# An inverse of 32 x 32 triangles moved from VectorE to TensorE, with more word buffers and a third load queue

## Chip, cores, metric

One core of a Trainium2 chip. The metric is the device time of one execution in microseconds (us). Ratios are the mean time of one kernel's fast runs over the mean of the other's from the same rounds, on the same chip, so they are not quite the ratio of the medians that stand beside them. Stretches within a kernel are read from one profiled execution each; whole times of one kernel differ by some 5 us either way between executions, so differences of a few us in a stretch are not read as effects.

Engine names as in the profile: PE is TensorE (matmuls), PEld its weight loads, DVE VectorE, ACT ScalarE, POOL GpSimd, SP SyncE. "issue" in a wait is time in which an engine waited for nothing that the profile shows.

## The reference, cut to what matters

```python
# block 1, for every token t of 768, 4 x 8 heads of 40 channels
y[t]  = r[t] @ state
Sa    = state @ a[t]
state = state * w[t] - outer(Sa, b[t]) + outer(v[t], k[t])
# block 2, on x = y laid out as (3072 tokens, 320)
h = x @ w_in            # 320 x 2048, given in double precision
out = (h * cos(h)) @ w_out
```

The kernel takes block 1 in 24 chunks of 32 tokens. In a chunk the recurrence becomes matmuls and the inverse of a 32 x 32 unit triangular matrix for each head. The weights of block 2 arrive as pairs of 32-bit words and are turned into f32 on the chip ("conversion", 36 blocks). Block 2's matmuls are laid between the chunks from chunk 2 on.

## The kernel before: what the change touches

The inverse of four chunks at once, 31 steps of two operations on VectorE:

```python
def inv_step(j):
    u, x = (G[n].rearrange("p (s t) -> p s t", s=C) for n in ("u", "inv"))
    tmp = ...
    nc.vector.tensor_tensor(tmp, u[:, :j, j : j + 1].to_broadcast([P, j, C - j]),
                            x[:, j : j + 1, j:].to_broadcast([P, j, C - j]), ALU.mult)
    nc.vector.tensor_tensor(x[:, :j, j:], x[:, :j, j:], tmp, ALU.subtract)
```

One block of conversion is a fetch from POOL, five operations on VectorE and two on ScalarE, cut into four steps (fetch, exponent, mantissa, product) that are laid between the segments of the chunks. Three word buffers rotate (`sb3`). The order ahead of the main loop:

```python
for seg in (v, k, g, *other[3:]):   # chunk 0's operands, then the triangles of chunks 2 and 3
    step(seg)
for work in inverse(0):             # the inverse of chunks 0 to 3, alone on VectorE
    work()
...
segs = [x, v, extra[0], s, k, extra[1], z, g, *extra[2:]]   # chunk 0; s is the first to use the inverse
```

## Time and profile before

| | before |
|---|---|
| median (4 runs) | 940.8 us (937.7 to 946.2) |
| profiled span | 937.8 us |
| PE busy | 775 us, 16472 matmuls |
| DVE busy | 537 us |
| instruction packets (queue q8) | 130, 2.13 MB |

How to read it: PE is the bound from about 213 us on; ahead of that DVE is the busier engine, with PE half idle. The lines of the page and of the stretches are in the prediction. I use these marks throughout, all read from PE's timeline: the first matmuls on the inverse (tile sps, 74.0 us before) and the first state transpose of chunks 1 to 5 (tile sT; chunk 5 at 274.8).

### The profile page before, as it was taken

Reading aid. Unit: us, or ns where it says so; the run is one execution under the profiler, and the core shown is the slowest. Engines: PE = TensorE matmul, PEld = TensorE weight load, DVE = VectorE, ACT = ScalarE, POOL = GpSimd, SP = SyncE. Lnnn points to the kernel's source line nnn. Section 1 sums busy time; section 2 is a strip of 40 time slices with the busy share of each in tenths; the row PEclk is TensorE's granted clock in tenths of the full one; section 3 lists DMA queues with packets and bytes.
Section 4 is the critical chain, followed back from the end, with each engine's and each line's share of the span. In section 5 each row is a group of like instructions: output and inputs, shape, how many; then the busy total and the mean of one; then the engine's idle time right before and its main releaser. Section 6 shows DMA issues by size and latency. Waiting matters only on the chain.

```text
span 937.8 us, 36893 instructions
## 1 busy us (share of the span) xinstructions
PE 775.1 (83%) x16472; PEld 598.6 (64%) x16472; DVE 536.5 (57%) x1178; ACT 357.0 (38%) x671; POOL 189.3 (20%) x372
## 2 busy tenths in 40 slices
PE   5604554758899899989889999999898999999997
PEld 4404443546677667777667777777676676777675
DVE  5499787797723567726468526588334765323322
ACT  1103433543433433534324443433434344534333
POOL 4303333131211122112022013023102202211000
PEclk9655555778999889999989999999999899999999
DMA  5432636230311411421420421312211112200000
GB/s 95 82 49 66 151 93 147 74 89 2 69 46 23 74 44 20 73 55 27 69 46 16 72 50 38 61 39 49 57 33 38 32 25 47 45 19 24 18 22 15
DMA packets 181471, 49.08 MB, mean 52 GB/s; under 512 B 159040, under 2 KB 179008, under 8 KB 181312
## 3 DMA queue, kind: packets, MB, share of 16 engines
q1 hardware_dynamic: 176192, 35.89, 20.0%
q0 software_dynamic: 2944, 10.49, 3.6%
q8 instruction: 130, 2.13, 0.9%
q10 hardware_dynamic: 2176, 0.33, 0.2%
q14 instruction: 29, 0.24, 0.1%
HBM read 38.80 MB, written 7.86 MB: 50 GB/s over the span
## 4 chain that ended last, share of the span: by engine, by line
PE 64%; DVE 18%; issue 6%; DMA 5%; ACT 4%; SPq 2%; POOL 1%; POOLq 0%; ACTq 0%; DVEq 0%
PE ph L101 24%; PE po L101 19%; PE x0ps L101 4%; DVE inv_tmp L384 3%; PE dps L101 3%; DVE inv L388 3%; DVE rw L330 2%; PE gram L101 2%; DVE turns L620 2%; SPq L149 2%; PE qps L101 2%; PE vT L273 2%; PE sT L468 2%; PE sps L101 2%; ACT turns L618 2%
## 5 line engine op out<-in xcount | busy, mean ns | idle before, releaser
L101 PE MATMUL po<-w_out_sb,gT 128*128 128x320 f32 x768 | 243.6, 465 | 0.0
L101 PE MATMUL ph<-xT,w_in_sb 128*128 128x256 f32 x768 | 193.2, 396 | 13.9 <-DVE gT L628 6.2
L620 DVE SCALAR_TENSOR_TENSOR turns<-turns,ph 128x512 f32<-128x512 f32 x96 | 61.7, 684 | 219.8 <-ACT turns L618 219.8
L101 PEld LDWEIGHTS po<-w_out_sb,gT 128*128 128x128 f32 x768 | 148.7, 203 | 58.5 <-issue 13.3
L101 PEld LDWEIGHTS ph<-xT,w_in_sb 128*128 128x128 f32 x768 | 143.1, 195 | 36.0 <-issue 13.3
L618 ACT ACTIVATE turns<-ph,rnd 128x512 f32<-128x512 f32 x96 | 60.8, 684 | 146.4 <-PE ph L101 146.4
L558 POOL TENSOR_TENSOR qz<-qz,wc 128x160 f32<-128x160 f32 x92 | 41.7, 470 | 346.0 <-DVE qz L557 345.3
L628 DVE TENSOR_TENSOR gT<-ph,turns 128x512 f32<-128x512 f32 x96 | 65.0, 684 | 18.3 <-ACT turns L625 18.0
L384 DVE TENSOR_TENSOR inv_tmp<-u,inv 128x31 f32<-128x31 f32 (+15 forms) x186 | 71.8, 386 | 4.2 <-POOL inv L371 0.4
L388 DVE TENSOR_TENSOR inv<-inv,inv_tmp 128x31 f32<-128x31 f32 (+15 forms) x186 | 69.5, 374 | 6.4
L625 ACT ACTIVATE turns<-turns,half_pi 128x512 f32<-128x512 f32 x96 | 69.3, 722 | 3.1
L624 ACT ACTIVATE turns<-turns 128x512 f32<-128x512 f32 x96 | 60.0, 625 | 8.4 <-DVE turns L620 8.4
L101 PE MATMUL ph<-xT,w_in_tail 64*128 64x256 f32 x384 | 54.8, 404 | 0.0
L330 DVE RECIPROCAL rw<-wn 128x320 f32<-128x320 f32 x24 | 51.6, 2150 | 2.1 <-PE wn L273 2.1
L101 PEld LDWEIGHTS ph<-xT,w_in_tail 64*128 64x128 f32 x384 | 33.3, 187 | 18.4 <-issue 15.6
L472 ACT COPY s<-sT 128x512 f32<-128x512 f32 x46 | 24.6, 588 | 46.1 <-PE sT L468 46.1
L273 PE MATMUL wT<-ident,nat_w 128*128 128x128 f32 x88 | 14.4, 315 | 32.2 <-DVE x L509 25.3
L557 DVE TENSOR_TENSOR qz<-dps,qz 128x160 f32<-128x160 f32 x92 | 29.1, 317 | 19.1 <-PE dps L101 19.0
L530 DVE TENSOR_TENSOR sm<-sps,su 128x128 f32<-128x128 f32 x48 | 14.0, 291 | 45.1 <-ACT sm L526 45.1
L273 PE MATMUL bT<-ident,bn 128*128 128x128 f32 x96 | 18.6, 327 | 25.3 <-ACT bT L343 18.7
L202 ACT ACTIVATE expo<-expo,to_bits 128x256 int32<-128x256 int32 (+1 forms) x36 | 19.2, 533 | 49.6 <-DVE expo L199 49.4
L468 PE MATMUL sT<-ident,qz 128*128 128x128 f32 x184 | 26.5, 288 | 11.4 <-DVE aT L332 11.4
(104 smaller groups left out, 1082.9 us busy)
## 6 DMA issues: line engine op xcount, KB each, us to landing
words<-in_moe_w_out_dram POOLq DMA_DIRECT2D x16, 320.0 KB, 3.7
words<-in_moe_w_in_dram POOLq DMA_DIRECT2D x16, 256.0 KB, 3.5
nat_k<-in_k_dram SPq DMA_DIRECT2D x96, 40.0 KB
nat_v<-in_v_dram SPq DMA_DIRECT2D x96, 40.0 KB
nat_r<-in_r_dram SPq DMA_DIRECT2D x96, 40.0 KB
xd<-yt SPq DMA_DIRECT2D x48, 80.0 KB
out_dram<-ot SPq DMA_DIRECT2D x24, 160.0 KB
nat_w<-in_w_dram SPq DMA_DIRECT2D x88, 40.0 KB
```

Of the source, the lines that this page charges most:

```text
L101: nc.tensor.matmul(o, lhsT=lhsT, rhs=rhs, start=start, stop=stop, skip_group_check=True)
L273: nc.tensor.transpose(ps[:, i * P : (i + 1) * P], x[:, 2 * i : 2 * i + 2].rearrange("p e d -> p (e d)"), ident)
L330: nc.vector.reciprocal(rw, unpad(ps[:, 0].rearrange("p (h d) -> p h d", h=H)))
L384: nc.vector.tensor_tensor(tmp, u[:, :j, j : j + 1].to_broadcast([P, j, C - j]), x[:, j : j + 1, j:].to_broadcast([P, j, C - j]), ALU.mult,)
L388: nc.vector.tensor_tensor(x[:, :j, j:], x[:, :j, j:], tmp, ALU.subtract)
L468: nc.tensor.transpose(ps[:, i // 4, (i % 4) * P : (i % 4 + 1) * P], qz[:, i // 2, i % 2, C : C + P], ident)
L558: nc.gpsimd.tensor_tensor(z, z, wc.rearrange("p (f m b) -> p f m b", f=2, m=2)[:, :, :, bb] .unsqueeze(3).to_broadcast([P, 2, 2, D]), ALU. ...
L618: nc.scalar.activation(n, u, ACTF.Identity, bias=rnd, scale=1.0)
L620: nc.vector.scalar_tensor_tensor(n, n, -ROUND, u, ALU.add, ALU.subtract)
L624: nc.scalar.activation(n, n, ACTF.Abs)
L625: nc.scalar.activation(n, n, ACTF.Sin, bias=half_pi, scale=-2.0 * math.pi)
L628: nc.vector.tensor_tensor(gT[:, 2 * e : 2 * e + 2].rearrange("p f t -> p (f t)"), us[e], ns[e], ALU.mult)
```

## The change

Its intent: get the 28 us of the first inverse off VectorE, so that conversion can begin earlier. The inverse of chunks 0 to 3 is made by repeated squaring, (1 + u)(1 + u^2)(1 + u^4)(1 + u^8)(1 + u^16), with u and its transpose l squared on TensorE. Conversion gets five word buffers (two of them in the still empty end of the w_out tile). The loads of a and b for chunks 2 and 3 go over POOL's queue. The padding memsets go to VectorE. The core of the diff:

```diff
+    def doubled(c, n):
+        u, l, q = (G[x][:, c * H : (c + 2) * H] for x in ("nt", "l", "q"))
+        work = [] if n == 4 else [("l", u, l)] if n == 3 else [("u", l, u), ("l", u, l)]
+        ...
+        for i, (_, left, right) in enumerate(work):
+            for h in range(2 * H):
+                for g in blk:
+                    mm(ps[g, i, h * C : (h + 1) * C], left[g, h, :], right[g, h, :], h == 0)
+        if n:
+            for g in blk:
+                mm(qps[g], ident[g, g], flat(q[g]), True)
+            for h in range(2 * H):
+                for g in blk:
+                    mm(qps[g, h * C : (h + 1) * C], l[g, h, :], q[g, h, :], False)
+        ...                                  # copies back by ScalarE
@@ words
-            t["words"] = sb3.tile([P, DM, 2], I32, tag="words", name="words")[:n, :wid]
+            if own(m):
+                words = sb3.tile([P, DM, 2], I32, tag="words", name="words")
+            else:
+                o = 2 * DM * (m % 5 - 3)
+                words = late_words[:, o : o + 2 * DM].rearrange("p (n w) -> p n w", w=2)
@@ loads
+    load(2, "a", nc.gpsimd)
+    load(3, "a", nc.gpsimd)
 ...
+        load(2, "b", nc.gpsimd)
+        load(3, "b", nc.gpsimd)
@@ order ahead of the loop
-        for seg in (v, k, g, *other[3:]):
-            step(seg)
-        for work in inverse(0):
-            work()
+        step(lambda: doubled(0, 0))
+        step(v, 0, 2)                        # 0, 2: two conversion steps after it
+        step(lambda: doubled(0, 1), 0, 2)
+        step(lambda: doubled(2, 0))
+        step(lambda: doubled(0, 2), 0, 2)
+        step(k)
+        step(lambda: doubled(2, 1), 0, 2)
+        step(lambda: doubled(0, 3))
+        step(g, 0, 2)
+        step(lambda: doubled(2, 2))
+        step(lambda: doubled(0, 4), 0, 2)
@@ chunk 0
-                segs = [x, v, extra[0], s, k, extra[1], z, g, *extra[2:]]
+                segs = [x, d3, s, v, d4, k, z, g, *extra]
```

## The prediction

> **What bounds the kernel now.** I read four views in this order: the page (for its slices), the table of stretches, the timeline of each engine for the first 260 us, and the waits of the start. From the page, slices of 23.4 us each:
>
> ```profile
> PE   5604554758899899989889999999898999999997
> DVE  5499787797723567726468526588334765323322
> PEclk9655555778999889999989999999999899999999
> ```
>
> From the tenth slice on PE is busy nine tenths of the time: there the kernel is bound by the matmuls of the second block, which the change does not touch. The first nine slices, some 210 us, are different: PE is half idle, its clock is at half, and DVE has the high digits. So a change to the start is worth the time by which the dense part begins earlier, and no more. I split the start at the marks where each chunk of the main loop begins (the first transpose of the state, from PE's timeline: chunk 1 at 106.8, 2 at 143.9, 3 at 197.7, 4 at 241.0). The columns are the busy time of PE, PEld, DVE, ACT and POOL, then clock, DMA share, GB/s:
>
> ```profile
> 73.50:106.80 33.30, 14.37 (x477) 11.66 (x477) 29.43 (x62) 11.79 (x26) 13.31 (x25) 0.50 0.39 104
> 106.80:143.90 37.10, 20.58 (x560) 17.34 (x557) 29.89 (x74) 14.95 (x33) 11.89 (x22) 0.50 0.46 116
> 143.90:197.70 53.80, 32.79 (x724) 25.90 (x725) 40.21 (x98) 25.61 (x48) 15.83 (x28) 0.63 0.41 100
> 197.70:241.00 43.30, 33.22 (x637) 25.71 (x636) 35.29 (x84) 17.01 (x33) 9.03 (x17) 0.88 0.17 42
> 241.00:278.00 37.00, 34.50 (x766) 26.40 (x767) 17.72 (x38) 15.18 (x28) 6.34 (x12) 0.95 0.30 56
> ```
>
> DVE is busy 88%, 81%, 75% and 82% of chunks 0 to 3; in chunk 4 it falls to 48% and PE takes over at 93%. The timeline of PE shows what lies ahead of chunk 0:
>
> ```profile
> 44.56 1.06 PE L273 MATMUL vT<-ident,rp 128*128 128x128 f32 x4
> 70.94 1.97 PE L273 MATMUL wT<-ident,nat_w 128*128 128x128 f32 x8 [25.31 <-DVE x L509]
> 73.97 1.25 PE L101 MATMUL sps<-x,rt 32*32 32x72 f32 x64 [1.06 <-ACT rT L425]
> ```
>
> PE stands still for 25.3 us while DVE does the inverse of chunks 0 to 3: transpose at 42.03, 31 pairs of operations, transpose back until 70.5, in all 28.5 us. DVE's timeline has no weight conversion before 70.8, although the first three blocks of words were fetched at 20.7. The conversion's 36 blocks then fill DVE until 213. Its groups in 70.5 to 213 add up to 77 us (18.7 + 16.2 + 13.2 + 13.1 + 7.4 + 6.9 + 1.7), so 2.1 us a block. DVE's own waits in that stretch, the longest:
>
> ```profile
> DVE mant L208 <- DMA words<-in_moe_w_in_dram: 5.8, 5, 2.0
> DVE mant L208 <- DMA words<-in_moe_w_out_dram: 4.0, 5, 1.9
> DVE turns L620 <- ACT turns L618: 3.0, 2, 2.0
> ```
>
> So 9.8 us are waits for words that three buffers could not fetch early enough.
>
> **What the Trainium skill says.** "TensorE: Matmul & The Clock Gate", section "What's actually happening": the array runs at half clock until it has been busy for a window of about 3.4 us. The trace agrees in kind: four transposes take 1.09 us at 18.2 and 0.60 us at 239, and the granted clock is 0.50 in chunks 0 and 1. But a dense run of small work at 104 to 113 us stayed slow (64 matmuls of qps took 1.94 us there, 1.14 us at 246.8), so I price the new products slow. "DMA: Bandwidth & Descriptors", section "Issuing engines are not separate DMA queues": a further queue saves only the issuer's time, all share 16 engines. Here that time matters: SP issues one load each 0.49 us, 52 of them from about 1 to 29 us, with the DMA share at 0.59. The same page, section "Anatomy of one DMA — SWDGE (gpsimd) path", says that many descriptors can be made before their cost shows. In the trace two-DMA fetches of 64 rows take POOL 0.52 us each and those of 128 rows 0.54 to 0.59, which agrees, but no DMA from POOL with 256 short runs, as now added, is in it. "GPSIMD Engine Reference", section "Specifications": POOL and DVE share their memory interface when DVE reads two inputs. The trace agrees: the mantissa operation took 1.37 us at 138.6, beside POOL's work on qz and yt, against 0.42 us alone.
>
> **The change part by part.**
>
> *Removed:* the 28.5 us of DVE and the 25.3 us hole of PE. Four loads each of a and b for two chunks (16) leave SP: 36 issues before the main loop in place of 52, so k, v, r of chunk 0 are issued by about 19 us in place of 26 to 29, and land 8 to 10 us earlier.
>
> *Added on PE:* for each of two pairs of chunks, seven products of 64 matmuls (2 + 2 + 2 + 1), and four updates of q (four matmuls with the identity over 512 columns, then 64). A product works on four diagonal tiles, 16 matmuls deep. From ph at the slow clock (eight matmuls of 256 columns in 3.78 us, 1.84 ns a column) 16 x 32 columns are 0.94 us; issue at nps's pace (128 in 1.64 us, 12.8 ns) would be 0.82. So 0.95 us a product and 0.95 + 0.95 = 1.9 us an update: 7 x 0.95 + 4 x 1.9 = 14.2 us a pair, 28.5 us for both; some 20 us if the clock rises. The two pairs alternate, with v (2.0), k (1.1), g (1.75) and x (1.25) between, so ACT's copies (0.59 us each, up to three a step) mostly hide and PE stays in step. PE's work up to the first use of the inverse is thus about 28.5 + 4 + 2 = 34 us. This lies on the path in place of the 28.5 us of DVE.
>
> *When it starts:* the first three steps keep their times (second bn at about 18.4). Then POOL issues eight loads of b: at 0.6 us, 5 us, to 23.3; three fetches, to 25; the bn of chunks 2 and 3 by 27.5. PE: bT, then nps of chunks 2 and 3 ends at about 31; DVE's mask and transposes (1 us a pair, estimated from the 2.09 us of the full one) by 33, POOL's q of the second pair at about 34, vp and rp after it at 34.6. PE then runs v at 35 and the doubling to about 61, x and the third step of the other pair to 66.5. So s of chunk 0 goes at about **66** in place of 74: 8 us earlier, 12 if the clock rises, and 0 if POOL's loads cost 1.5 us each.
>
> *Moved:* conversion. Before s of chunk 0 there are now 12 steps of the list in the prologue and four each in x and d3: 20 steps, five blocks in place of two. The loop of chunk 0 has 13 segments in place of 11, so at the start of chunk 1 there are 12 + 13 x 4 = 64 steps done (16 blocks) against 44 (11 blocks), a lead of five blocks that stays.
>
> *Sum, in two ways.* (1) DVE from s of chunk 0 to the last conversion at 213: 23.4 + 18.5 + 22.0 + 15.7 + 20.8 + 11 = 111 us busy in 138, or 81%. Three blocks fewer: 105. At 81% this takes 130 us, at 87% (the 9.8 us of waits for words gone, thanks to five buffers) 121. From 66 it ends at 187 to 196: **17 to 26 us** earlier. (2) By chunks: after s, chunk 0 has 11 segments where it had 8, DVE work 31 + 6 = 37 us, so chunk 1 starts at about 105, hardly earlier than 106.8, but five blocks ahead; chunk 1 loses some 3 us of waits and chunk 2 starts at about 139; chunk 2 has 9 blocks left in place of 14, of which 11 fell in it before: 4 us of DVE and 3 of waits less, chunk 3 at about 186 in place of 197.7; chunk 3 loses its last three blocks, 6 us, and chunk 4 starts at about 223 in place of 241: **18 us**. After that PE is the bound and the lead is carried to the end unchanged. The memsets that move from POOL to DVE (some 20 of 0.21 us, 4 us) fall into DVE's idle time from 2.8 to 9.3 and cost nothing.
>
> I take the middle of both with a little for a risen clock and for POOL: its waits for the last operation of a conversion are the longest of the start (80.9 us), and fetches that are placed one block later stop it less. That makes **22 us**, so 937.9 - 22 = **916 us**.
>
> **The rivals.**
>
> *A: the path is only exchanged.* 34 us of PE at the slow clock replace 28.5 us of DVE, and chunk 0 is longer by three segments. For it: way (2) has chunk 1 starting almost when it did. Against: the five blocks and the waits are real DVE time in stretches where DVE is 75 to 88% busy. It would give 925 to 930.
>
> *B: the third queue costs more than it saves.* If POOL takes 1.5 us or more for a load of 256 runs, the 16 take 24 us; bn of chunk 2 comes at 33 or later and s of chunk 0 where it was. Only the five blocks remain: 10 to 12 us, about 926. Against: the flat 0.52 to 0.59 us.
>
> *C: DVE is the only bound.* With DVE filled from 36 us on, its 115 us would end at 151 and the gain would reach 60 us. Against: the prologue hands it only three blocks in 30 us, and the order of each engine is fixed; but dense PE work that raises the clock early and a freer POOL could give 30 to 35 us, 903 to 908.
>
> **Range and chances.** A and B set the upper end, 928, C the lower, 900. The line for over 2% is 937.9 x 0.98 = 919.1, which lies 3 us above my middle. I put A and B together at about a third, the rest at or below 918, and slower at next to nothing, since nothing is added after chunk 0. Faster 0.64, same 0.34, slower 0.02.
>
> **What would show each step right or wrong.** The first matmuls on rt (tile sps) should start at 62 to 70 us; the new products should take 0.8 to 1.0 us each, less if the clock view shows over 0.5 there. POOL's load issues should be at 0.55 to 0.8 us. The fifth conversion should be done by sps, the waits of the mantissa for words should fall below 3 us, the last conversion should be near 190, and the state's first transpose in chunk 4 near 220. From there to the end 697 us should remain, as before. The prediction is wrong if chunk 4 starts within 8 us of 241 (A or B), before 208 (C), or if that last stretch changes by over 5 us.

## More of the kernel before

A helper issues every small matmul. For f32 data **one call makes two MATMUL and two LDWEIGHTS instructions**: `p1_n` calls it 2 x 4 x 4 x 2 = 64 times and the profile counts nps x128.

```python
def mm(o, lhsT, rhs, start, stop=True):
    nc.tensor.matmul(o, lhsT=lhsT, rhs=rhs, start=start, stop=stop, skip_group_check=True)
```

## The result, and the profile after

The changed kernel is **slower: 992.2 us** (987.7 to 992.6, 4 runs) against 940.8; ratio 1.053, interval 1.046 to 1.060. The page of the changed kernel:

```profile
span 990.3 us, 42636 instructions
...
PE   4656655467989999999899988898998899999997
...
DVE  7400198978862638833467625477433576223222
...
PEclk8757766567999989999989999999999899999999
...
q8 instruction: 152, 2.49, 1.1%
```

The slices are 24.8 us here. In slices 3 to 5 (49.5 to 124 us) DVE stands at 0, 0 and 1: it no longer makes the inverse, but it is idle, not at work on conversion. PE shows five or six tenths there. The last line is the queue that brings instructions: packets, MB, share. Before it was

```profile
q8 instruction: 130, 2.13, 0.9%
```

so 22 packets and 0.36 MB more, 16.4 KB a packet. The marks (us), from PE's timelines:

| | sps, chunk 0 | chunk 1 | chunk 2 | chunk 3 | chunk 4 | chunk 5 | end |
|---|---|---|---|---|---|---|---|
| before | 74.0 | 106.8 | 143.9 | 197.7 | 241.0 | 274.8 | 937.8 |
| after | 120.6 | 158.6 | 191.1 | 243.7 | 275.4 | 309.6 | 990.3 |
| later by | 46.6 | 51.8 | 47.2 | 46.0 | 34.4 | 34.8 | 52.5 |

Three things have to be explained: 46.6 us lost before the inverse is used, 12 us won back by chunk 4, and 17.7 us lost after chunk 5, where the code is the same.

The first shows in PE's timeline of the changed kernel. The columns are start, duration, engine, line, operation, tiles, shapes, count, and in brackets the idle time before it and what ended it:

```profile
55.30 1.87 PE L103 MATMUL ulps<-nt,l 32*32 32x32 f32 x124 [1.67 <-issue]
...
58.75 1.87 PE L103 MATMUL ulps<-l,nt 32*32 32x32 f32 x124 [1.53 <-issue]
...
62.76 1.88 PE L103 MATMUL ulps<-nt,l 32*32 32x32 f32 x124 [2.08 <-issue]
...
66.76 1.87 PE L103 MATMUL ulps<-l,nt 32*32 32x32 f32 x124 [2.07 <-issue]
```

A product is 128 matmuls, not 64, and takes 1.87 us at this clock. Then PE waits 1.5 to 2.1 us for nothing the profile shows, and the next begins. The period is 3.5 to 4.0 us. The waits of PE from 33.1 us to sps (in total, times, longest) show no engine and no transfer that it waited for; all of its 33 idle us have the mark "issue":

```profile
PE ulps L103 <- issue: 24.9, 13, 2.7
PE qps L103 <- issue: 6.1, 6, 1.9
PE gram L103 <- issue: 2.0, 1, 2.0
```

DVE's timeline of the same kernel shows that it does not use the time:

```profile
46.19 0.42 DVE L229 SCALAR_TENSOR_TENSOR mant<-words,mant 128x256 f32<-128x256 uint32 x1
76.17 0.42 DVE L238 SCALAR_TENSOR_TENSOR expo<-words,expo 128x256 int32<-128x256 int32 x1 [29.55 <-ACT expo L222]
...
97.51 0.42 DVE L516 TENSOR_TENSOR ag<-gram,su 128x256 f32<-128x256 f32 x1 [20.46 <-PE gram L103]
```

DVE waits 29.6 and 20.5 us. In the first wait its next conversion step needs ScalarE, and ScalarE in the order of the program first waits to copy products out; in the second the next in DVE's order needs `gram`, which PE reaches only then. The stretch from the first product to sps, and the next ones to chunk 5 (columns as in the prediction):

```profile
33.10:120.55 87.45, 54.39 (x2951) 42.55 (x2950) 12.79 (x31) 16.50 (x33) 8.02 (x13) 0.62 0.17 35
120.55:158.63 38.08, 18.97 (x652) 14.98 (x639) 32.88 (x70) 16.24 (x35) 13.91 (x26) 0.67 0.46 114
158.63:191.14 32.51, 19.48 (x563) 16.57 (x557) 29.90 (x74) 15.13 (x34) 11.05 (x21) 0.60 0.43 108
191.14:243.65 52.51, 33.78 (x725) 26.61 (x726) 41.44 (x96) 24.25 (x45) 14.40 (x25) 0.64 0.35 78
243.65:275.44 31.79, 30.21 (x637) 23.67 (x636) 25.79 (x60) 12.56 (x24) 6.57 (x13) 1.00 0.17 35
275.44:309.59 34.15, 31.07 (x748) 23.68 (x749) 16.90 (x36) 14.10 (x26) 4.78 (x10) 0.95 0.32 56
```

In the first, 87 us for what I had put at 34: PE is busy 54 us and idle 33, DVE is busy 13. Of the later stretches chunk 1 is 4.6 us shorter than before and chunk 3 is 11.5 us shorter; chunk 0 is 5.2 us longer counted from sps, with three more segments in it.

**The theory** that I then held: PE waits for its own instructions. The change adds 1440 calls, each two matmuls and two weight loads, so 5760 instructions. Divided by the 22 further packets that is 262 a packet, close to 256 instructions of 64 bytes in 16.4 KB. "Advanced Engine Details and Errata" of the Trainium skill, section "ISA Cache", states just this size: a line of 16 KB holds 256 instructions. I had not looked it up. A block of 256 is used up in one burst of 128 loads and matmuls, and the next is not there.

The packets of q8 in the trace have times; they bear the theory out. Each packet is 16384 bytes. In the changed kernel 23 of them start between 32.9 and 116.8 us, one each 3.3 to 4.6 us (mean 3.8), though a packet itself takes 1.2 us. PE has 17 gaps of over 0.8 us between 33 us and sps, and every one ends 1.2 to 1.6 us after the end of such a packet. So the gaps end when a block has come. The cycle, in medians, is: a burst begins, 1.1 us later the next packet starts, it takes 1.2 us, and 1.4 us after its end the next burst begins. In all 14 traces together no two packets of q8 start within 3.2 us of each other.

**Rivals:** the products are simply slow at the half clock and their order (product, copy, product) leaves gaps; or the queue, buffers and new order of the change cost the time; and for the 17.7 us at the end, something else in the change, such as the new shapes of the PSUM tiles.

### The profile page after: what moved, and what is told of

The parts are those of the page before. It is cut to its first block, busy times and chain, and to the rows that moved or that the text cites. A ratio compares the mean times of both kernels' runs of the same rounds, so it can differ in the third digit from the quotient of the medians.

```text
span 990.3 us, 42636 instructions
## 1 busy us (share of the span) xinstructions
PE 826.5 (83%) x19352; PEld 638.7 (64%) x19352; DVE 519.4 (52%) x1136; ACT 368.1 (37%) x693; POOL 195.5 (20%) x373
## 4 chain that ended last, share of the span: by engine, by line
PE 67%; DVE 13%; issue 10%; ACT 4%; DMA 3%; POOL 2%; SPq 0%; POOLq 0%; DVEq 0%; ACTq 0%
PE ph L103 22%; PE po L103 20%; PE qps L103 4%; PE x0ps L103 3%; PE gram L103 3%; PE ulps L103 3%; DVE rw L355 2%; PE dps L103 2%; DVE turns L686 2%; PE vT L293 2%; PE sT L533 2%; PE sps L103 2%; ACT turns L684 2%; DVE wb L334 1%; PE nps L103 1%
## 5 line engine op out<-in xcount | busy, mean ns | idle before, releaser
L103 PE MATMUL ph<-xT,w_in_sb 128*128 128x256 f32 x768 | 197.3, 403 | 15.4 <-DMA xT<-xd 7.2
L103 PEld LDWEIGHTS ph<-xT,w_in_sb 128*128 128x128 f32 x768 | 146.0, 199 | 38.2 <-issue 14.6
L449 DVE TENSOR_TENSOR inv_tmp<-u,inv 128x31 f32<-128x31 f32 (+15 forms) x155 | 59.7, 385 | 2.9
L453 DVE TENSOR_TENSOR inv<-inv,inv_tmp 128x31 f32<-128x31 f32 (+15 forms) x155 | 57.9, 374 | 5.3
L595 DVE TENSOR_TENSOR sm<-sps,su 128x128 f32<-128x128 f32 x48 | 14.0, 291 | 49.5 <-ACT sm L591 49.4
L293 PE MATMUL bT<-ident,bn 128*128 128x128 f32 x96 | 16.7, 302 | 24.9 <-ACT bT L368 17.1
L634 POOL TENSOR_TENSOR yt<-yt,wb 128x512 f32<-128x512 f32 x24 | 31.0, 1291 | 22.1 <-DVE yt L629 22.1
L533 PEld LDWEIGHTS sT<-ident,qz 128*128 128x128 f32 x184 | 22.6, 150 | 16.9 <-issue 10.7
```

Source lines behind the costliest of these rows:

```text
L293: nc.tensor.transpose(ps[:, i * P : (i + 1) * P], x[:, 2 * i : 2 * i + 2].rearrange("p e d -> p (e d)"), ident)
L533: nc.tensor.transpose(ps[:, i // 4, (i % 4) * P : (i % 4 + 1) * P], qz[:, i // 2, i % 2, C : C + P], ident)
```

## The experiments

All runs were correct. All executions were fast but one of e12's six (936.4 us), which is left out of its ratio; its median is 927.4 without it. Marks as above, from the profile of each run:

| run | median us | ratio to before | sps | chunk 5 | sps to chunk 5 | chunk 5 to end | packets |
|---|---|---|---|---|---|---|---|
| before | 940.8 | 1 | 74.0 | 274.8 | 200.8 | 663.0 | 130 |
| the change | 992.2 | 1.053 | 120.6 | 309.6 | 189.0 | 680.7 | 152 |
| e1_dve_inverse | 926.7 | 0.981 | 69.9 | 261.5 | 191.6 | 661.2 | 130 |
| e2_half_issue | 952.2 | 1.009 | 81.9 | 270.5 | 188.5 | 680.0 | 141 |
| e3_pad_before | 949.4 | 1.005 | 73.6 | 268.1 | 194.5 | 677.2 | 130 |
| e4_pad_after | 975.3 | 1.033 | 116.3 | 307.6 | 191.3 | 666.4 | 153 |
| e5_fill | 979.7 | 1.041 | 120.7 | 300.3 | 179.6 | 679.6 | 152 |
| e6_joint | 933.9 | 0.995 | 73.7 | 265.3 | 191.6 | 661.6 | 140 |
| e7_joint_fill | 934.7 | 0.994 | 77.9 | 267.7 | 189.8 | 665.6 | 140 |
| e8_three_buffers | 939.5 | 0.998 | 69.6 | 271.2 | 201.7 | 662.1 | 130 |
| e9_joint_early | 939.2 | 0.997 | 93.7 | 269.3 | 175.7 | 668.3 | 140 |
| e10_joint_even | 931.5 | 0.989 | 79.2 | 260.9 | 181.7 | 667.6 | 140 |
| e11_pad16 | 935.0 | 0.997 | 73.3 | 263.5 | 190.2 | 669.8 | 130 |
| e12_pad48 | 928.3 | 0.986 | 69.7 | 259.0 | 189.3 | 661.6 | 130 |

### e1: the change without the squaring

```diff
-        step(lambda: doubled(0, 0))
-        ...
+        for seg in (v, k, g):
+            step(seg)
+        for work in inverse(0):
+            work()
```

> The changed kernel with the first inverse back on VectorE (31 pairs of operations), all else of the change kept. Theory (the products on TensorE are the whole loss, the other parts help as predicted): the first matmuls on rt (sps) start at 64 to 68 us in place of 120.6 in the changed kernel and 74.0 before, TensorE has no run of issue gaps before them, and the time is 915 to 930 us. Rival (third queue, word buffers or new order lose time too): time above 938 us and sps after 74 us.

Measured: 926.7 us, ratio 0.981 (0.975 to 0.987). Sps is at 69.9, some 2 us later than expected and 4 earlier than before. The whole loss goes with the squaring; the rest of the change helps. The rival about queue and buffers falls.

### e2: half the instructions, the same columns

```diff
-            for h in range(2 * H):
+            for h in range(0, 2 * H, 2):
                 for g in blk:
-                    mm(ps[g, i, h * C : (h + 1) * C], left[g, h, :], right[g, h, :], h == 0)
+                    mm(ps[g, i, h * C : (h + 2) * C], left[g, h, :], flat(right[g, h : h + 2, :]), h == 0)
```

and the same in the update of q. Half the heads get the wrong weights. That it still passed as correct suggests that the second and higher powers of u are too small in this data for the check to see (not tested further); it is no usable kernel.

> Wrong result on purpose: in the new products and updates each small matmul takes two heads' columns (64 in place of 32) with one head's weights, so the array passes the same columns with half the instructions: 704 calls, 2816 TensorE instructions fewer, 11 instruction blocks of 16 KB at 256 instructions each. Theory (TensorE waits for its instructions, one block per 3.9 us): sps of chunk 0 at 75 to 85 us in place of 120.6, some 43 us earlier, instruction packets 141 in place of 152, and the time about 945 to 955 us. Rival (the columns at the slow clock are the cost): a burst keeps its 1.9 us per 2048 columns and the gaps stay, sps not before 105 us.

Measured: sps at 81.9, so 38.6 us earlier for 11 blocks, 3.5 us a block, with 141 packets as counted. This is what the instruction theory said, at the edge of its numbers. The columns alone do not set the time. But the run is not as clean as I had meant it: with fewer gaps the clock rose too. PE's timeline of e2:

```profile
46.86 1.04 PE L103 MATMUL ulps<-l,nt 32*32 32x64 f32 x60 [1.86 <-issue]
...
47.75 1.04 PE L103 MATMUL ulps<-nt,l 32*32 32x64 f32 x60
...
51.14 1.04 PE L103 MATMUL ulps<-l,nt 32*32 32x64 f32 x60 [2.29 <-issue]
```

3840 columns take 1.04 us here, against 1.87 us for 3968 in the change, and the mean granted clock from 33 us to sps is 0.89 against 0.62. So part of a burst's length was the clock. What does not depend on it is the block: from 46.86 to 51.14, two bursts of 64 and one wait, 4.3 us for about 256 instructions, although they ran in 2 us. With the faster clock the burst was shorter and the wait filled the rest: q8's packets from 33 us to sps start each 3.9 us on average, against 3.8 in the change.

### e3, e4, e11, e12: where the block borders fall

The squaring adds 5760 instructions, 22.5 blocks. So all later borders shift by half a block against the instructions. To move them alone, idle matmuls on the identity are put at the very start, where PE waits for data (32 calls, 128 instructions, for half a block):

```diff
+        pad = ps_h.tile([P, 512], F32, tag="h", name="pad")
+        for i in range(32):
+            mm(pad[blk[i % 4], :C], ident[blk[i % 4], blk[i % 4]], ident[blk[i % 4], blk[i % 4]], True)
         for seg in first[:3]:
             step(seg)
```

e3 does this to the kernel before (with ph's PSUM tile written as 512 columns, as in the change), e4 to the changed kernel, e11 and e12 with 16 and 48 calls to e1.

> The kernel before with 32 idle small matmuls (128 TensorE instructions, half an instruction block) put ahead of the first transposes, where TensorE waits for data, so that block borders move by half a block; the change moves them by 22.5 blocks, the same phase. Theory (the 17.7 us that the changed kernel loses after chunk 5 come from where the borders fall): from the first state transpose of chunk 5 to the end about 675 to 682 us in place of 663.0, time about 950 us. Rival (they come from other parts of the change): 661 to 666 us and time 936 to 942 us.

> The changed kernel with the same 32 idle matmuls, which bring the block borders of the later chunks back to where they are in the kernel before. Theory of the borders: chunk 5 to the end falls from 680.7 to 661 to 668 us, time about 975 us. Rival: 678 to 683 us, time 990 us or a little more.

> e1_dve_inverse with 16 idle small matmuls (64 TensorE instructions, a quarter of an instruction block) at the start. Theory of the block borders: chunk 5 to the end is again another value than at 0 (661 to 666 us) and at half a block (677 to 681 us), within 655 to 690 us, and the time follows it. Rival (only the half block matters by chance of one kernel): 661 to 666 us, as without.

> As e11_pad16 with 48 idle matmuls, three quarters of a block. Theory: chunk 5 to the end moves away from 661 to 666 us; if one of the quarter places is lower, it gives the fastest kernel of the study, below 925 us. Rival: 661 to 666 us.

Measured, chunk 5 to the end: before 663.0, with half a block 677.2; the change 680.7, with half a block more 666.4. Both go as the border theory said, in both directions. e2 (736 calls, 11.5 blocks more than before) and e5 (22.5) are half a block off too, at 680.0 and 679.6; e1, e6 and e8, off by whole blocks, are at 661 to 662, and e7, e9 and e10 (also whole blocks, with conversion laid elsewhere) at 666 to 668. e3 also has the new shape of ph's PSUM tile; but e1 has it too, at 661.2, so the rival of the PSUM shapes falls. So the 17.7 us at the end are a side effect of how many instructions stand ahead, not of what they do. The waits of PE from chunk 5 on, first of the kernel before, then of e3 (in total, times, longest):

```profile
PE x0ps L101 <- issue: 6.0, 3, 2.1
...
PE gram L101 <- issue: 2.2, 1, 2.2
```

```profile
PE gram L101 <- issue: 7.5, 4, 2.2
PE x0ps L101 <- issue: 7.2, 4, 2.0
```

More borders fall into dense runs of small matmuls, and each costs some 2 us. That is 6.5 us of the 14.2 between these two. From the change to e4 the same two lines fall from 14.7 to 7.3 us, of 14.3. PE's own work from chunk 5 to chunk 23 also takes longer, 552.0 in place of 546.3 us, at a mean clock of 0.96 in place of 0.97; the rest I have not traced. In e3 the time up to chunk 5 got 6.7 us shorter, so the total moved by 0.5% only, within the 950 expected but from two changes that partly cancel.

The quarter places are not settled: 669.8 for 16 calls lies just above the 661 to 668 of all kernels that are off by whole blocks, 661.6 for 48 lies in it, against the expectation that it would move away. Neither beats e1: 0.997 and 0.986 against 0.981.

### e5: conversion beside the products

Conversion steps after the eleven parts ahead of the loop: (8, 4, 12, 8, 12, 4, 12, 8, 4, 12, 8), 92 in all, in place of 12.

```diff
-        step(lambda: doubled(0, 0))
-        ...
+        for work, n in zip(
+            (lambda: doubled(0, 0), v, lambda: doubled(0, 1), lambda: doubled(2, 0),
+            ...
+            (8, 4, 12, 8, 12, 4, 12, 8, 4, 12, 8),
+        ):
+            step(work, 0, n)
```

> The changed kernel, with 92 conversion steps (23 blocks) in place of 12 (3 blocks) laid beside the products on TensorE ahead of chunk 0. Theory (TensorE waits for instructions there and VectorE is idle, so conversion costs nothing): sps of chunk 0 stays at 118 to 124 us, and from there to chunk 5 it takes 135 to 160 us in place of 189, so the time falls to 945 to 965 us. Rival (the steps hold up the copies that the products wait for, or conversion was not the bound after sps): sps after 130 us, or sps to chunk 5 above 175 us; time above 975 us.

Measured: sps at 120.7, unmoved, with DVE busy 49 us of that stretch in place of 13. So PE's wait is not DVE's or ACT's doing, and conversion was free there. But sps to chunk 5 fell only from 189.0 to 179.6, 9.4 us for 20 blocks, and the time is 979.7: both are numbers of the rival (above 175, above 975), in its second form, that conversion was not the bound after sps. Here a block of conversion done early was worth 0.5 us, not its 2.1 us of DVE time.

### e6, e7: the same squaring in 640 calls

u and q are laid side by side, so one matmul of 64 columns with the weights l gives both l^T u and l^T q; the new l is the transpose of the new u, by VectorE; q is added by VectorE.

```diff
+        for h in range(2 * H):
+            for g in blk:
+                mm(pv[g, h, part].rearrange("p w t -> p (w t)"), l[g, h, :],
+                   uq[g, h, part].rearrange("p w t -> p (w t)"), h % H == 0)
+        if n < 4:
+            nc.scalar.copy(uq[:, :, 0], pv[:, :, 0])
+            nc.vector.transpose(l, uq[:, :, 0])
+        if n:
+            nc.vector.tensor_tensor(dst, pv[:, :, 1], uq[:, :, 1], ALU.add)
```

> The changed kernel with the same repeated squaring in 640 calls in place of 1440: u and q lie side by side so that one matmul of 64 columns makes both, the transpose l is made by VectorE from u, and q is added by VectorE. 3200 TensorE instructions fewer, 12.5 blocks. Theory (instructions set the pace, 3.9 us a block): sps of chunk 0 at 70 to 78 us in place of 120.6, some 46 us earlier; with the borders back in phase (c5 to end 661 to 667 us) the time is 922 to 935 us. Rival (the dependence of the steps on one another is as long as the instruction supply): sps above 90 us, time above 945 us.

> e6_joint with 60 conversion steps (15 blocks) in place of 12 (3 blocks) beside the products. Theory: sps at 70 to 82 us, sps to chunk 5 at 160 to 172 us in place of 189, time 898 to 918 us, better than all before it. Rival (VectorE's transposes and additions of the squaring now stand behind the conversion): sps above 95 us and time no better than e6_joint.

Measured, e6: sps at 73.7, 46.9 us earlier for 12.5 blocks, 3.75 us a block, and 661.6 us from chunk 5 on. Time 933.9, ratio 0.995. PE's waits from 33 us to sps, where the change had 24.9 us in its first line:

```profile
PE ulps L103 <- issue: 11.0, 6, 2.5
```

This settles the first and the third of the three questions: the same mathematics with fewer instructions takes away the loss, at the price of a block that was seen in the trace, and the end comes back with the phase. (e8 answers the second.) e6 is still no better than the inverse on VectorE.

e7 has 15 blocks of conversion in the prologue in place of 3. Sps at 77.9, but 189.8 us to chunk 5, and 934.7 us: the theory's gain failed, and the rival's sps above 95 did not come either. Chunk 0 took 43.2 us, in which DVE was busy 38.3:

```profile
77.89:121.04 43.15, 20.01 (x635) 16.86 (x625) 38.33 (x83) 16.94 (x36) 13.96 (x26) 0.54 0.51 121
121.04:156.56 35.52, 19.09 (x562) 16.44 (x557) 25.25 (x63) 12.52 (x28) 9.02 (x18) 0.56 0.23 64
```

Each segment of chunks 0 and 1 brings a block of conversion, wanted or not, and chunk 0 is bound by DVE. What had been moved ahead was replaced by what came next.

### e9, e10: where conversion should lie

e9 has 92 steps in the prologue and one a segment in chunk 0, two in chunk 1; e10 has e7's 60 and two in both.

```diff
-            fill = (1, 4 if c < 2 else 3)
+            fill = (1, (2, 2, 3)[min(c, 2)])        # e10; e9: (1, 2, 3)
```

> The joint squaring (e6) with 92 conversion steps (23 blocks) beside it and one step a segment in chunk 0, two in chunk 1, in place of four. Theory (a block costs some 0.35 us beside the products, from e7 against e6, but about 2 us in chunk 0, where VectorE is 89% busy): sps at 78 to 84 us, chunk 0 falls from 43 to 26 to 32 us, chunk 5 begins at 245 to 258 us, time 908 to 922 us. Rival (chunk 0 is bound by the order of its small steps, not by VectorE): chunk 0 stays above 38 us and the time at 930 us or more.

> e7_joint_fill with two conversion steps a segment in chunks 0 and 1 in place of four; 15 blocks beside the squaring as there. Theory: sps at 76 to 80 us as in e7, chunk 0 at 30 to 35 us, last conversion in chunk 2, chunk 5 begins at 252 to 262 us, time 914 to 926 us. Rival: what chunks 0 and 1 gain, chunk 2 loses in full, and the time stays at e7's 933 us.

Measured: e10 has chunk 0 at 35.5 us, chunk 1 at 26.9, chunk 2 at 50.6 (42.4 in e7), chunk 5 at 260.9; 931.5 us, ratio 0.989 (0.986 to 0.992). Chunk 5 comes 6.8 us earlier than in e7, but the ratios (0.994 there, 0.988 to 1.000) are not clear of each other, and the time is 5 us over the theory's: of the 16 us that chunks 0 and 1 gain on e7, chunk 2 gives 8 back. e9 missed: chunk 0 took 32.0 us, within the theory's range, but sps came only at 93.7 and the time is the rival's. There PE waits for DVE inside the squaring, which now uses DVE itself; the waits of PE from 33 us to sps in e9:

```profile
PE ulps L103 <- DVE uq L440: 11.9, 3, 5.6
PE ulps L103 <- DVE rt L440: 4.2, 1, 4.2
PE ulps L103 <- issue: 3.9, 2, 2.4
```

The rival named for e7 holds in e9: the additions of the squaring stand in DVE's queue behind conversion.

### e8: three buffers again

```diff
-    own = lambda m: m >= 3 * NW // 4 or m % 5 < 3
+    own = lambda m: True
```

> e1_dve_inverse with three word buffers as before the change (third queue and new order kept). Theory (the buffers are worth the waits for words, some 9 us): time 3 to 9 us above e1_dve_inverse, sps at 68 to 71 us as there, VectorE's waits for words back to about 10 us. Rival (the buffers are worth nothing): within 2 us of e1_dve_inverse.

Measured: sps at 69.6 as in e1, but 201.7 us to chunk 5 in place of 191.6, time 939.5 against e1's 926.7 (they ran on different chips; their ratios to the kernel before are 0.998 and 0.981). DVE's waits for words, from sps on in e8:

```profile
DVE mant L222 <- DMA words<-in_moe_w_in_dram: 4.9, 5, 1.7
DVE mant L222 <- DMA words<-in_moe_w_out_dram: 4.0, 3, 2.3
```

In e1 no such line is left. The buffers are worth some 10 us, all of the gain that e1 has in sps to chunk 5. The time is 13 us over e1's median, more than the 3 to 9 expected, but from another chip. This also explains most of the 12 us won back by chunk 4: sps to chunk 4 takes 167.1 us before, 167.7 in e8, 157.8 in e1 and 154.9 in the change. The third queue and the new order bring sps 4 us forward, which e8's ratio does not show clear of noise.

## Why the prediction was wrong

**The bound, right.** DVE bounded the start and PE the rest; e1 and e8 show that easing DVE there shortens the time.

**Loads and queue, right.** POOL's loads of 256 runs took 4.62 us for eight, 0.58 each, against my 0.6, and rival B did not come. In e1, with the inverse on VectorE, sps came at 69.9, 4 us earlier than before; the prediction's 66 was for the products on TensorE.

**"Added on PE", wrong: the step that failed.** I wrote 0.95 us a product, 1.9 us an update, 28.5 us for both pairs, 34 us up to sps. It took 87.5. Two errors lie in it. I priced the 64 calls of a product at the profile's pace for 64 single matmuls (nps, 12.8 ns) and at ph's 1.84 ns a column, though each call is two matmuls: a product then is 1.88 us at the slow clock, as the 1.87 us measured, and the sum doubles from 28.5 to 57 us. PE was busy 54.4 us in that stretch. The other 33 us are the second error, PE's waits for instructions: I took the rate of short groups (nps, 12.8 ns a matmul) for one that can be held. A group of 128 with slow large matmuls around it finds its instructions ready; 2880 in a row do not. They need 22.5 blocks, and e2 and e6 put a block at 3.5 to 3.75 us, together 79 to 84 us of the 87.5. e2 shows that a faster clock (0.89) does not help: there too a packet came each 3.9 us. My rival A had the right place but only 6 us of it. The page before has "issue" with 6% of its chain, and the prediction does not ask what that is.

**"Moved", partly right.** The lead of five blocks did arise, but is worth 2.6 us (sps to chunk 5: 189.0 with it, 191.6 in e1 without, a difference within the noise), not 10. The sum (1) treated DVE's busy time as additive on the path; e5 measured 0.5 us a block. That the buffers bring 10 us was right, and with e1's last conversion at 198 us, against 187 to 196 in the sum, its size was not far off, for another reason.

**"The lead is carried to the end unchanged", wrong.** The last stretch after chunk 5 grew by 17.7 us, because 22.5 blocks moved the borders by half a block. e3 and e4 show it. The prediction's own test ("if that last stretch changes by over 5 us") caught it, without a cause in mind.

**A reading of the clock.** The four transposes of 1.09 us at 18.2, which the prediction sets against the half clock, lie before the trace's first clock record (26.5 us), where the view shows 1.00. Those at 108.7, also 1.09 us, lie in a stretch at 0.50 and bear the point out.

**Left open:** why the next block is asked for only 1.1 us after a burst begins, too late to hide, how the 14 to 18 us of a bad phase split beyond the 6.5 us of waits, and whether a quarter block matters.

The best version is e1: everything of the change except the squaring, 1.9% faster than before (1.3 to 2.5%, so that over 2% is not shown). Its interval overlaps with those of e12 and e10.

## What to carry to other kernels

Before moving work to TensorE as many tiny matmuls, count instructions, not columns: here two matmuls and two weight loads for each f32 call, and some 3.5 to 4 us for each 256 of them in a long run, whether a matmul had 32 or 64 columns. Look at "issue" gaps after a fixed number of instructions and at the packets of the instruction queue; merge operands that share weights before anything else. And when code that was not touched changes its time, move its instruction blocks by a few idle instructions before looking for a cause in the change.

## What the Trainium skill lacked or had wrong

- "Advanced Engine Details and Errata", section "ISA Cache", has the line of 16 KB and 256 instructions, which the 22 packets of 16.4 KB for 5760 instructions agree with. It lacks the rate: in a long run of small matmuls PE got a block only each 3.3 to 4.6 us (mean 3.8), with gaps of up to 2.7 us, though a packet took 1.2 us. "Runtime: NRT & Kernel Launch" has a section on instruction fetch ("Instruction fetch mechanics"), which this text does not rest on; a rate for such a run is missing there too.
- "TensorE: Matmul & The Clock Gate", section "Back-to-back issue gap", gives rates by column count and, for up to 64 columns, a floor of about 25 ns a matmul. Here, with four 32 x 32 tiles side by side, a burst ran below it, at 15 ns a matmul (124 in 1.87 us), but the long run above it: 2951 pairs of load and matmul in 87.5 us, about 30 ns a pair. Instruction supply as a limit is not named in that section.
- None of the pages cited here says that the position of block borders changes the time of unchanged code: 663.0 against 677.2 us and 680.7 against 666.4 us for 128 idle instructions.
- That one f32 matmul call becomes two matmul and two load instructions here (64 calls of nps, counted x128) stands on none of the pages cited here.
